# Attention with an MLP behind it: only TensorE's instructions kept in the order of the source, and the MLP's groups dealt out by TensorE's time

## The chip, the core and the metric

The kernel runs on one core of a Trainium2 chip. A core has five engines that run side by side, each with its own queue of instructions in a fixed order: TensorE (PE; its weight loads are shown apart, as PEld), VectorE (DVE), ScalarE (ACT), GpSimd (POOL) and SyncE (SP), whose queue here does nothing but issue transfers. An instruction waits by semaphores for what it needs, and all that stand behind it on its engine wait with it. The metric is the time of one execution on the device, in microseconds.

## The reference

Eight batches, eight heads of width 64, 576 positions. Attention is causal by blocks of 64 positions; its output, with the heads side by side (576 x 512), goes through a gated MLP with a layer norm and a mixing over positions.

```python
scores = np.matmul(q, k.transpose(0, 1, 3, 2)) / np.sqrt(D)
scores = np.where(block_i >= block_j, scores, -1e9)          # blocks of 64
attn = np.exp(scores - scores.max(-1, keepdims=True))
attn = attn / (attn.sum(-1, keepdims=True) + 1e-9)
x = np.matmul(attn, v)                    # then heads side by side: (B, S, 512)
h = np.maximum(x @ w_in, 0.0)             # (B, S, 1024)
u, v = h[..., :512], h[..., 512:]
v_n = (v - mean(v)) / np.sqrt(var(v) + 1e-6)
v_s = np.einsum('ts,bsd->btd', w_spatial, v_n) + b_spatial[None, :, None]
return (u * v_s) @ w_out
```

## The kernel before

The kernel walks through 32 pairs of heads (8 batches of 4 pairs), and each pair through 7 slots. Slot 0 is the last 64 queries of both heads; slots 1 and 2 are query tiles 0 and 1 of the first and the second head, slots 3 and 4 tile 2, slots 5 and 6 tile 3. A step is one slot of one pair. The loop of steps writes the instructions of all engines in one order.

Products are made in a fast fp32 form with rounded inputs, and so each operand is split in two: hi is the rounded value (a cast on ScalarE, L244), lo the rest (a subtraction on GpSimd, L247). Three matmuls (hi by hi, hi by lo, lo by hi) stand for one. prep_pair splits the q and k of a pair, with two casts and then four pieces of lo. There is one buffer for the loaded data (`raw`), one for hi and one for lo. The pairs of batch 0 (the boot) are not split: their scores are full fp32, and their probabilities are turned over by TensorE (transposes_pe).

Of a split pair TensorE does, in this order: the scores of slots 0, 1 and 2 (L295, L283); MLP groups of the batch before; the scores of slots 3 to 6; the weighted-value product of the pair two before (av, L464 and L481, "AV" below); more MLP groups. The scores of a slot go through VectorE (row maximum, L318 and L327), ScalarE (exp, L334), VectorE (reciprocal of the sum, L345 and L348) and GpSimd (norm, L352). VectorE turns the probabilities over within blocks of 32 (transposes, L408) into a buffer `q`, and 16 transfers on SP's queue (move, L422) bring these blocks to their places in `turned`, of which there is one. av reads `turned`, so the next pair's moves wait for it to end.

AV gives x, in hi and lo (L439 on ScalarE, L443 on VectorE). When the four x of a batch are there, its MLP is put in a queue as groups of matmuls: v groups (mv, L512), u groups (mu, L606), sp groups (ms, the mixing over positions, L630) and out groups (mo, L664). Each has an evacuation and further work on the other engines, put off by later(steps, phase, ...) to a phase of a later step; due(phase) writes what has come due. `rate` is the number of groups over the number of steps, and each step that has a whole credit takes one group.

The splitting of a pair, and in batches 0 and 1 that of the weights, is background work: spread(generator, pieces, first, last) deals it out over steps.

What sets the order of each engine is own(): it pins each instruction behind the one pinned before it on the same engine. Every compute instruction is pinned. The transfers of SP are not: where they stand in its queue is decided by the tile scheduler, which puts instructions in the order in which it reckons that they can start.

Of the kernel before, what the change touches and what calls it, by code (L numbers as in the profile page):

```python
# [29 lines left out]
NS = len(SLOTS)  # L30
# [3 lines left out]
RUN2 = 3  # L34
AV_AT, BOOT_AV = 2 * NS + RUN2, NS + 5

# [6 lines left out]
def kernel(  # L43
# [10 lines left out]
    nc = tc.nc  # L54
# [5 lines left out]
    ND = DH // P  # L60
# [19 lines left out]
    def own(ins):  # L80

        tc.keep_in_program_order(ins)

# [350 lines left out]
    def x_evac(b, pr, av, q0, n):  # L434
        qs = slice(q0, q0 + n)

        def hi():
            x = x_tiles(b, pr)
            own(nc.scalar.copy(x[:, 0, qs], av[:, :n]))  # L439

        def lo():
            x = x_tiles(b, pr)
            own(nc.vector.tensor_tensor(  # L443
                out=x[:, 1, qs], in0=av[:, :n], in1=x[:, 0, qs].bitcast(F32), op=ALU.subtract
            ))

        later(1, 0, hi)
        later(1, 1, lo)

    def av(b, pr):  # L450
# [27 lines left out]
        for c in range(5):  # L478
# [9 lines left out]

        later(1, 2, lambda: own(nc.gpsimd.tensor_scalar(
            out=tails[b][:, pr], in0=xts[(b, pr)][:, :, FULL * P:].bitcast(F32), scalar1=1.0,  # L490
# [4 lines left out]
    def moe(b):  # L495
# [5 lines left out]
        def v_group(c):  # L501
# [89 lines left out]

            later(1, 0, evac)
            later(1, 2, stats)
            later(2, 1, scale)
            later(2, 2, normal)
            later(3, 2, rest)

        def u_group(z, dc):
# [17 lines left out]

            later(1, 0, evac)

# [3 lines left out]
        def sp_group(z, dc):  # L622
# [30 lines left out]

            later(1, 0, gate)
            later(1, 1, split_g)

        def out_group(z, ec):
# [16 lines left out]

            later(1, 0, leave)

        def groups(f, need, *args):
            return [(need, lambda a=a: f(*a)) for a in args]

        def free():  # L680
            return True

        vs = groups(v_group, free, *((c,) for c in range(FULL + 1)))
        us = groups(u_group, free, *((z, d) for z in range(2) for d in range(ND)))
        sps = [groups(sp_group, lambda: ready["v"] > FULL, *((z, d) for d in range(ND)))
               for z in range(2)]
        outs = [groups(out_group, lambda z=z: ready[z] == ND, *((z, e) for e in range(NO)))
                for z in range(2)]

        order = "vvuvuvuvuuuuu" if b else "v" * 5 + "u" * 8  # L690
        queue = [(vs if w == "v" else us).pop(0) for w in order]
# [59 lines left out]
    queue = []  # L751
    rate = 0.0
    credit = 0.0

# [12 lines left out]
    def begin(b):  # L767
        nonlocal rate
        queue.extend(moe(b))
        steps = NPAIR * NS + (0 if b else AV_AT - BOOT_AV)  # L770
        rate = len(queue) / steps if b < B - 1 else 1.0

    n = -1
    while n < N + NS or queue or todo:
# [5 lines left out]
        if here and g + 1 < len(pairs):  # L780
            b, pr = pairs[g + 1]
            if i == 0 and b > 0:
                load_pair(b, pr)
            if i == NS - 1 and b == 0 and pr > 1:
                load_v(b, pr)
            if n == 1:
                load_pair(0, 1)
                load_v(0, 1)
            if i == RUN2 + 1 and g + 2 < NPAIR:
                load_pair(0, g + 2)  # L790
            if i == RUN2 + 1 and b > 0:
                spread(prep_pair(b, pr), 6, n, n + 2)
        if i == 3 and NPAIR < g < len(pairs):
# [15 lines left out]
        for of in range(max(0, g - 2), min(g + 1, len(pairs))):  # L809
            b, pr = pairs[of]  # L810
            if n - of * NS == (BOOT_AV if by_pe((b, pr)) else AV_AT):
                av(b, pr)
                if pr == NPAIR - 1:
                    later(1, 3, lambda b=b: begin(b))

# [16 lines left out]
        step_background(n)  # L832
        if at(n - 4) and by_pe(at(n - 4)[:2]):
            for j in TURNS[(i - 4) % NS]:
                transposes_pe(*at(n - 4)[:2], j)
        credit = min(credit + rate, 2.0)
        while credit >= 1.0 and queue and queue[0][0]():
            queue.pop(0)[1]()
            credit -= 1.0
        due(2)  # L840
# [46 lines left out]
```

## Time and profile before

| | us |
|---|---|
| median of three runs | 800.57 |
| the three runs | 791.61, 800.57, 807.21 |
| the profiled execution | 797.51 |
| its span in the trace | 795.7 |
| granted TensorE clock over the span | 0.935 |

The profile is of one execution. A row of an engine gives its busy time, the share of the span and the number of instructions. A row of waits names who waited, for whom, the sum in us, the number of times and the longest. A row of a timeline begins with the start and the duration in us; in brackets stands how long the engine had been idle, and what ended it. The granted clock is a share of full speed. Names are those of the program: `s` scores, `p` probabilities, `q` the turned blocks, `lo` and `hi` the halves of q and k.

### The profile page before, as it was taken

The page shows a single profiled execution, that of the slowest core. Times are in us where ns is not written, and L with a number is a line of the kernel's source. Part 1 is how long each engine was busy: PE and PEld are TensorE (multiplying, and loading weights), DVE is VectorE, ACT ScalarE, POOL GpSimd, SP SyncE. Part 2 cuts the span into 40 slices and gives each one's busy share as a digit, 9 for nine tenths or more (in the row PEclk, how much of TensorE's full clock was granted, in tenths as well). Part 3 has the DMA queues.
Part 4 walks back from the last instruction along what each step waited for, and adds up shares of the span by engine and source line. Part 5 has one row for each costly group of instructions (what it writes and reads, how often), then busy time and mean ns, then how long its engine had stood idle before and what let it go on. Part 6 is the DMA issues. An engine that isn't in the chain of part 4 may idle for free.

```text
span 795.7 us, 16364 instructions
## 1 busy us (share of the span) xinstructions
PE 715.7 (90%) x5729; PEld 635.5 (80%) x5729; DVE 465.2 (58%) x1587; ACT 426.4 (54%) x1156; POOL 342.6 (43%) x529
## 2 busy tenths in 40 slices
PE   8876968898988898998988899988988989899998
PEld 5554757787888787887878788887878988799898
DVE  5657877754774557745684557745675456731430
ACT  5775574443663457634763457634664437642542
POOL 4557467642444543344434543355344434341011
PEclk9997877989998999999998999999989889899999
DMA  7322445334444454345444354444544344431001
GB/s 259 123 72 93 128 126 157 88 116 136 124 116 130 127 157 112 105 123 146 130 130 130 101 165 115 113 115 139 152 129 102 97 121 132 98 99 36 26 1 60
DMA packets 42150, 92.05 MB, mean 116 GB/s; under 512 B 9298, under 2 KB 18002, under 8 KB 42068
## 3 DMA queue, kind: packets, MB, share of 16 engines
q1 hardware_dynamic: 32852, 81.56, 37.8%
q10 hardware_dynamic: 9216, 9.44, 3.5%
q8 instruction: 45, 0.74, 0.4%
q14 instruction: 37, 0.30, 0.1%
HBM read 38.18 MB, written 9.44 MB: 60 GB/s over the span
## 4 chain that ended last, share of the span: by engine, by line
PE 66%; POOL 13%; DVE 9%; issue 5%; ACT 4%; DMA 2%; SPq 1%; POOLq 0%; DVEq 0%; ACTq 0%
PE mo L664 10%; PE ms L630 10%; PE mu L606 10%; PE s L283 9%; PE mv L512 9%; POOL lo L247 7%; PE avh L464 6%; POOL p L352 4%; PE s L295 3%; PE avl L464 3%; DVE p L318 2%; PE avh L481 2%; DVE q L408 2%; ACT p L334 1%; PE t L380 1%
## 5 line engine op out<-in xcount | busy, mean ns | idle before, releaser
L334 ACT ACTIVATE p<-p,nmax 128x384 f32<-128x384 f32 (+4 forms) x288 | 167.3, 582 | 207.0 <-DVE nmax L318 97.0
L352 POOL TENSOR_SCALAR p<-p,ssum 128x384 f32<-128x384 f32 (+4 forms) x288 | 161.5, 575 | 197.9 <-DVE ssum L348 166.0
L247 POOL TENSOR_TENSOR lo<-raw,hi 128x288 fp32r<-128x288 f32 x112 | 95.3, 872 | 110.4 <-issue 89.0
L318 DVE CUSTOM_DVE_ANT_0 p<-s,mask 128x128 f32<-128x128 f32 (+3 forms) x256 | 117.3, 481 | 21.0 <-PE t L380 13.9
L606 PE MATMUL mu<-x,wi_hi 128*128 128x288 f32 x512 | 119.9, 316 | 0.0
L408 DVE STREAM_TRANSPOSE q<-p 128x384 f32<-128x384 f32 (+1 forms) x189 | 108.6, 612 | 16.7 <-POOL p L352 8.2
L649 POOL TENSOR_TENSOR gl<-u,gh 128x288 fp32r<-128x288 f32 x64 | 51.7, 809 | 110.5 <-ACT gh L648 110.5
L639 DVE TENSOR_TENSOR u<-ms,u 128x288 f32<-128x288 f32 x64 | 29.2, 456 | 116.2 <-PE ms L635 116.2
L606 PEld LDWEIGHTS mu<-x,wi_hi 128*128 128x128 f32 x512 | 91.9, 204 | 3.7 <-issue 0.9
L512 PE MATMUL mv<-wi_hi,x 128*128 128x512 f32 x256 | 84.5, 397 | 0.0
L630 PE MATMUL ms<-ws_hi,vh 128*128 128x288 f32 x256 | 82.7, 323 | 0.2 <-ACT q L386 0.2
L630 PE MATMUL ms<-ws_lo,vh 128*128 128x288 f32 x256 | 79.6, 311 | 0.0
L630 PE MATMUL ms<-ws_hi,vl 128*128 128x288 f32 x256 | 79.6, 311 | 0.0
L664 PE MATMUL mo<-gh,wo_hi 128*128 128x288 f32 x256 | 77.8, 304 | 0.0
L664 PE MATMUL mo<-gl,wo_hi 128*128 128x288 f32 x256 | 76.8, 300 | 0.0
L664 PE MATMUL mo<-gh,wo_lo 128*128 128x288 f32 x256 | 76.7, 299 | 0.0
L295 PE MATMUL s<-hi,lo 128*128 128x288 f32 x56 | 22.3, 399 | 59.4 <-POOL lo L247 59.4
L606 PE MATMUL mu<-x,wi_lo 128*128 128x288 f32 x256 | 75.4, 314 | 0.0
L295 PEld LDWEIGHTS s<-hi,lo 128*128 128x128 f32 x56 | 12.7, 227 | 64.5 <-POOL lo L247 64.5
L512 PEld LDWEIGHTS mv<-wi_hi,x 128*128 128x128 f32 x256 | 48.4, 189 | 10.8 <-issue 0.6
L630 PEld LDWEIGHTS ms<-ws_hi,vh 128*128 128x128 f32 x256 | 52.4, 205 | 3.0 <-issue 1.3
L334 ACT ACTIVATION_READ_ACCUMULATOR p<-p,nmax 128x1 f32 x288 | 54.3, 189 | 0.0
(118 smaller groups left out, 1620.7 us busy)
## 6 DMA issues: line engine op xcount, KB each, us to landing
turned<-q SPq DMA_DIRECT2D x216, 100.0 KB, 2.2
turned<-q SPq DMA_DIRECT2D x216, 96.0 KB, 2.2
raw<-qk SPq DMA_DIRECT2D x31, 608.0 KB, 4.1
v<-v SPq DMA_DIRECT2D x32, 320.0 KB, 4.3
outT<-o ACTq DMA_DIRECT2D x64, 144.0 KB, 1.8
rwi<-w_in SPq DMA_DIRECT2D x8, 512.0 KB, 4.3
rwo<-w_out SPq DMA_DIRECT2D x4, 512.0 KB, 4.4
rws<-w_spT SPq DMA_DIRECT2D x4, 288.0 KB, 3.1
```

What stands on the lines that cost most here:

```text
L247: own(nc.gpsimd.tensor_tensor(out=lo[:, cs], in0=raw[:, cs], in1=hi[:, cs].bitcast(F32), op=ALU.subtract))
L283: own(nc.tensor.matmul(banks[(b, pr, i + hd)][:, o:o + n], a[js, qs], k[js, :n], start=(m == 0), stop=(m == len(parts) - 1),))
L295: own(nc.tensor.matmul(bk[z][:, :HT], a[:, Q8:], k[:, z * HT:(z + 1) * HT], start=(m == 0), stop=(m == len(parts) - 1),))
L318: own(nc.vector.tensor_tensor_reduce(out=pt[:, o:o + n], in0=bk[:, o:o + n], in1=mask[:, 512 - n:], scale=-0.125, scalar=BIG, op0=ALU.add, ...
L334: own(nc.scalar.activation(pt[:, o:o + n], pt[:, o:o + n], AF.Exp, bias=mx, scale=-1.0, accum_out=ssum[:, s0 + r:s0 + r + 1],))
L352: own(nc.gpsimd.tensor_scalar(out=pt[:, o:o + w], in0=pt[:, o:o + w], scalar1=ssum[:, r:r + 1], scalar2=1.0, op0=ALU.mult, op1=ALU.mult,))
L408: own(nc.vector.transpose(to[:, :, o:o + 32 * n].rearrange("p r (c j) -> p c r j", j=32), pt[:, :n * P].rearrange("p (c r j) -> p c r j", ...
L464: own(nc.tensor.matmul(out[js, (t0 - q0) * P:(t1 + 1 - q0) * P].rearrange("p (t a j) -> p a t j", a=4, j=32), vt[:, c, js], src[:, :, o:o ...
L512: own(nc.tensor.matmul(ps, xs[k][:, j, cs], w[:, k, DH:], start=(n == 0), stop=(n == 3 * NC - 1),))
L606: own(nc.tensor.matmul(ps[:, :HT], w[:, k, ds], xs[k][:, j, zs], start=(n == 0), stop=(n == 3 * NC - 1),))
L630: own(nc.tensor.matmul(ps[:, :HT], a[:, ds], w[:, k, zs], start=(n == 0), stop=False))
L664: own(nc.tensor.matmul(ps[:, :HT], w[:, k, es], a[:, k, :], start=(n == 0), stop=(n == 3 * ND - 1),))
```

## The change

own() now pins only TensorE's instructions. The scheduler orders the four other engines, and SP's queue as before, by its own reckoning. TensorE's order is written a little differently too. MLP groups are dealt out by their length on TensorE: each has a number (in us), each step pays `pace` in, a group or a fixed part of a pair (PAIR_LENGTHS: scores of slots 0 to 2, scores of 3 to 6, AV) takes its length out. The phases of several evacuations move back by one, and so does the start of a batch's MLP. The first split pair, (1, 0), is prepared from slot 2 over four steps instead of from slot 4 over two. In the boot AV and the transposes come one step sooner, and one v group changes places with a u group.

```diff
-AV_AT, BOOT_AV = 2 * NS + RUN2, NS + 5
+AV_AT, BOOT_AV = 2 * NS + RUN2, NS + 4
+
+PAIR_LENGTHS = (1.8, 1.45, 2.95)
...
     def own(ins):
 
-        tc.keep_in_program_order(ins)
+        if ins.ins.engine == mybir.EngineType.PE:
+            tc.keep_in_program_order(ins)
...
-        later(1, 0, hi)
-        later(1, 1, lo)
+        later(1, 1, hi)
+        later(1, 2, lo)
...
-            later(1, 0, evac)
+            later(1, 1, evac)
             later(1, 2, stats)
             later(2, 1, scale)
             later(2, 2, normal)
-            later(3, 2, rest)
+            later(3, 1, rest)
...
-            later(1, 0, gate)
-            later(1, 1, split_g)
+            later(1, 1, gate)
+            later(1, 2, split_g)
...
-        vs = groups(v_group, free, *((c,) for c in range(FULL + 1)))
-        us = groups(u_group, free, *((z, d) for z in range(2) for d in range(ND)))
+        vs = groups(v_group, 2.75, free, *((c,) for c in range(FULL + 1)))
+        us = groups(u_group, 1.6, free, *((z, d) for z in range(2) for d in range(ND)))
...
-        order = "vvuvuvuvuuuuu" if b else "v" * 5 + "u" * 8
+        order = "vvuvuvvuuuuuu" if b else "v" * 5 + "u" * 8
...
-        rate = len(queue) / steps if b < B - 1 else 1.0
+
+        pace = (sum(q[2] for q in queue) + sum(PAIR_LENGTHS) * steps / NS) / steps
...
-            if i == RUN2 + 1 and b > 0:
-                spread(prep_pair(b, pr), 6, n, n + 2)
+            if i == (2 if boot else RUN2 + 1) and b > 0:
+                spread(prep_pair(b, pr), 6, n, n + (4 if boot else 2))
...
-                    later(1, 3, lambda b=b: begin(b))
+                    later(2, 1, lambda b=b: begin(b))
...
-        if at(n - 4) and by_pe(at(n - 4)[:2]):
-            for j in TURNS[(i - 4) % NS]:
-                transposes_pe(*at(n - 4)[:2], j)
-        credit = min(credit + rate, 2.0)
-        while credit >= 1.0 and queue and queue[0][0]():
-            queue.pop(0)[1]()
-            credit -= 1.0
+        if at(n - 3) and by_pe(at(n - 3)[:2]):
+            for j in TURNS[(i - 3) % NS]:
+                transposes_pe(*at(n - 3)[:2], j)
+        if here and not boot and i in (0, RUN2):
+            owed -= PAIR_LENGTHS[0] if i == 0 else PAIR_LENGTHS[1]
+        if i == RUN2 and NPAIR + 1 < g < len(pairs):
+            owed -= PAIR_LENGTHS[2]
+        owed = min(owed + pace, 3.0)
+        while owed > 0.0 and queue and queue[0][0]():
+            _, group, length = queue.pop(0)
+            group()
+            owed -= length
```

How this moves instructions is seen in the built programs. In the rows below a name carries batch, pair and slot: p_4_2_3 is the probabilities of batch 4, pair 2, slot 3. Lines of the changed kernel are three higher than before.

The first place is the split of pair (4, 3), done during pair (4, 2). ScalarE's row of instructions before, from the exp of slot 3 on:

```order
L334 ACTIVATE p_4_2_3_4925,ssum_4_2_3_4924<-p_4_2_3_4925,nmax_4_2_3_4923 128x384
L566 ACTIVATE vr_3_2_4814<-vr_3_2_4814,st_3_2_4815 128x512
L574 CAST vh_3_2_4947<-vr_3_2_4814 128x512
L439 CAST x_4_0_4950<-avl_4_0_4880 128x256
L439 CAST x_4_0_4950<-avh_4_0_4881 128x320
L530 ACTIVATE vr_3_3_4932<-mv_3_3_4931 128x512
L334 ACTIVATE p_4_2_4_4960,ssum_4_2_3_4924<-p_4_2_4_4960,nmax_4_2_4_4959 128x384
L244 CAST hi_4_3_4965<-raw_4_3_4736 128x576
L244 CAST hi_4_3_4965<-raw_4_3_4736 128x640
```

and in the changed kernel:

```order
L337 ACTIVATE p_4_2_3_4924,ssum_4_2_3_4923<-p_4_2_3_4924,nmax_4_2_3_4922 128x384
L569 ACTIVATE vr_3_2_4813<-vr_3_2_4813,st_3_2_4814 128x512
L337 ACTIVATE p_4_2_4_4940,ssum_4_2_3_4923<-p_4_2_4_4940,nmax_4_2_4_4939 128x384
L577 CAST vh_3_2_4932<-vr_3_2_4813 128x512
L247 CAST hi_4_3_4948<-raw_4_3_4736 128x576
L247 CAST hi_4_3_4948<-raw_4_3_4736 128x640
L442 CAST x_4_0_4944<-avl_4_0_4879 128x256
L337 ACTIVATE p_4_2_5_4977,ssum_4_2_5_4976<-p_4_2_5_4977,nmax_4_2_5_4975 128x512
L442 CAST x_4_0_4944<-avh_4_0_4880 128x320
```

The two casts of hi_4_3 stood behind the x of the AV and an evacuation of a v group (vr_3_3); now they stand right behind the exp of slot 4 and a cast of vh, ahead of both. GpSimd at the same place before:

```order
L247 TENSOR_TENSOR lo_4_3_4966<-raw_4_3_4736,hi_4_3_4965 128x288 x2
L489 TENSOR_SCALAR xs_4_4951<-x_4_0_4950 128x128
L352 TENSOR_SCALAR p_4_2_3_4925<-p_4_2_3_4925,ssum_4_2_3_4924 128x384
L352 TENSOR_SCALAR p_4_2_4_4960<-p_4_2_4_4960,ssum_4_2_3_4924 128x384
L247 TENSOR_TENSOR lo_4_3_4966<-raw_4_3_4736,hi_4_3_4965 128x288
L247 TENSOR_TENSOR lo_4_3_4966<-raw_4_3_4736,hi_4_3_4965 128x352
```

and in the changed kernel:

```order
L355 TENSOR_SCALAR p_4_2_3_4924<-p_4_2_3_4924,ssum_4_2_3_4923 128x384
L355 TENSOR_SCALAR p_4_2_4_4940<-p_4_2_4_4940,ssum_4_2_3_4923 128x384
L250 TENSOR_TENSOR lo_4_3_4949<-raw_4_3_4736,hi_4_3_4948 128x288 x3
L250 TENSOR_TENSOR lo_4_3_4949<-raw_4_3_4736,hi_4_3_4948 128x352
L355 TENSOR_SCALAR p_4_2_5_4977<-p_4_2_5_4977,ssum_4_2_5_4976 128x512
```

The four pieces of lo_4_3 stood two and two around the tail's copy (xs) and two norms; now the norms come first and all four pieces follow.

The second place is SP's queue one pair earlier. Before, from the last moves of q_4_0 on:

```order
L422 DMA turned_122<-q_4_0_4310 32x800 x2
L422 DMA turned_122<-q_4_0_4310 32x768 x2
L234 DMA raw_4_3_4736<-qk 128x1216
L256 DMA v_4_1_4861<-v 128x640
L422 DMA turned_122<-q_4_1_4593 32x768
```

and in the changed kernel, up to the first moves of q_4_0:

```order
L259 DMA v_4_0_4567<-v 128x640
L237 DMA raw_4_3_4736<-qk 128x1216
L425 DMA turned_122<-q_4_0_4322 32x768
L425 DMA turned_122<-q_4_0_4322 32x800 x2
L425 DMA turned_122<-q_4_0_4322 32x768
```

The load of raw_4_3 stood behind all sixteen moves of q_4_0; now it stands ahead of them.

The third place is VectorE at the end of pair (4, 2), up to the first row maximum of pair (4, 3), nmax_4_3_0. Before:

```order
L582 TENSOR_TENSOR vl_3_3_5025<-vr_3_3_4932,vh_3_3_5024 128x512
L536 TENSOR_TENSOR vr_3_4_5013<-mv_3_4_5012,vr_3_4_5013 64x512
L539 TENSOR_SCALAR vr_3_4_5013<-vr_3_4_5013 64x512
L542 BN_STATS st_3_4_5014<-vr_3_4_5013 64x6
L543 BN_AGGR st_3_4_5014<-st_3_4_5014 64x2
L546 TENSOR_SCALAR st_3_4_5014<-st_3_4_5014 64x1
L408 STREAM_TRANSPOSE q_4_2_4914<-p_4_2_3_4925 128x3x4x32
L408 STREAM_TRANSPOSE q_4_2_4914<-p_4_2_4_4960 128x3x4x32
L345 TENSOR_SCALAR ssum_4_2_5_4997<-ssum_4_2_5_4997 128x2
L348 RECIPROCAL ssum_4_2_5_4997<-ssum_4_2_5_4997 128x2
L327 ISA p_4_3_0_5090,nmax_4_3_0_5088<-s_4_3_0_0_5060,mask_93 128x288
```

and in the changed kernel:

```order
L411 STREAM_TRANSPOSE q_4_2_4913<-p_4_2_6_5011 128x4x4x32
L545 BN_STATS st_3_3_4956<-vr_3_3_4955 128x6
L546 BN_AGGR st_3_3_4956<-st_3_3_4956 128x2
L549 TENSOR_SCALAR st_3_3_4956<-st_3_3_4956 128x1
L539 TENSOR_TENSOR vr_3_4_4991<-mv_3_4_4990,vr_3_4_4991 64x512
L555 TENSOR_SCALAR st_3_3_4956<-st_3_3_4956 128x1
L542 TENSOR_SCALAR vr_3_4_4991<-vr_3_4_4991 64x512
L559 TENSOR_SCALAR st_3_3_4956<-st_3_3_4956 128x1
L545 BN_STATS st_3_4_4992<-vr_3_4_4991 64x6
L563 TENSOR_SCALAR st_3_3_4956<-st_3_3_4956 128x1
L546 BN_AGGR st_3_4_4992<-st_3_4_4992 64x2
L330 ISA p_4_3_0_5074,nmax_4_3_0_5072<-s_4_3_0_0_5044,mask_93 128x288
```

Before, the statistics of one v group (st_3_4) and two transposes of slots 3 and 4 came ahead of it; now the last transpose of the pair (slot 6) and the statistics of two v groups (st_3_3, st_3_4) do.

## What the change should do to the time

> **What bounds the kernel now.** I read the totals and the chain of waits first, since they say which engine to follow, and then the waits of that engine.
>
> ```profile
> span 795.7 us, 16364 instructions
> PE 715.7 (90%) x5729; PEld 635.5 (80%) x5729; DVE 465.2 (58%) x1587; ACT 426.4 (54%) x1156; POOL 342.6 (43%) x529
> PE 66%; POOL 13%; DVE 9%; issue 5%; ACT 4%; DMA 2%; SPq 1%; POOLq 0%; DVEq 0%; ACTq 0%
> PE s L295 <- POOL lo L247: 61.5, 26, 4.8
> PE avl L464 <- DMA turned<-q: 2.2, 1, 2.2
> ```
>
> TensorE is busy for 90% of the span, and of its 80 us of idle time 61.5 us are one wait: the first scores of a split pair wait for GpSimd's low halves, in 26 places. The transfers into `turned` cost it 2.2 us in all. So the time can fall by about 10% and no more, unless the matmuls themselves become faster, and the windows by stage (length, busy time of PE, its weight loads, DVE, ACT and POOL, granted clock, DMA share, GB/s) say that they can, a little.
>
> ```profile
> 0.00:57.10 57.10, 48.03 (x347) 31.36 (x347) 32.38 (x134) 37.73 (x109) 27.71 (x52) 1.00 0.46 152
> 57.10:130.20 73.10, 56.10 (x358) 46.17 (x357) 57.20 (x171) 45.25 (x116) 46.09 (x56) 0.81 0.42 117
> 130.20:683.50 553.30, 505.17 (x4189) 457.10 (x4189) 340.83 (x1181) 297.98 (x821) 246.20 (x390) 0.94 0.46 126
> 683.50:795.70 112.20, 106.35 (x839) 100.83 (x837) 34.81 (x103) 45.48 (x113) 22.60 (x34) 0.97 0.17 48
> ```
>
> I cut the span where pairs begin: A is the boot batch with the first three split pairs (to 130.2), B the 24 pairs from there (553.3 us, 92.2 us for each four pairs), C the last pair and the tail. In A's second part and in B the granted clock is 0.81 and 0.94. The next rows show what a lost clock looks like: a wait for the low half, then matmuls at 0.44 us where such ones take 0.29.
>
> ```profile
> 249.01 0.61 PE L295 MATMUL s<-hi,lo 128*128 128x288 f32 x1 [2.32 <-POOL lo L247]
> 254.41 0.44 PE L630 MATMUL ms<-ws_lo,vh 128*128 128x288 f32 x1
> 255.90 0.29 PE L630 MATMUL ms<-ws_hi,vh 128*128 128x288 f32 x1
> 249.00:256.00 7.00, 6.99 (x34) 6.49 (x35) 1.39 (x6) 1.19 (x3) 2.84 (x4) 0.53 0.55 165
> 273.60:280.60 7.00, 6.99 (x54) 6.46 (x54) 4.17 (x18) 2.86 (x10) 3.58 (x5) 1.00 0.57 182
> ```
>
> A seven-microsecond stretch behind the 2.32 us wait ran at 0.53, another, behind a wait as long, at 1.00: the loss follows some of the waits. In B it is 0.06 x 553 = 33 us.
>
> One batch in full, and its first pair, where TensorE's weighted-value product (AV) starts at 304.74:
>
> ```profile
> 295.30:384.40 89.10, 81.76 (x706) 74.00 (x705) 56.39 (x198) 50.12 (x138) 40.06 (x64) 0.98 0.47 127
> 318.35 0.40 PE L295 MATMUL s<-hi,lo 128*128 128x288 f32 x1 [2.39 <-POOL lo L247]
> 339.48 0.40 PE L295 MATMUL s<-hi,lo 128*128 128x288 f32 x1 [2.32 <-POOL lo L247]
> 362.66 0.40 PE L295 MATMUL s<-hi,lo 128*128 128x288 f32 x1 [2.63 <-POOL lo L247]
> 304.74 0.87 PE L464 MATMUL avl<-turned,v 128*64 128x256 f32 x8
> 310.73 0.60 ACT L530 ACTIVATE vr<-mv 128x512 f32<-128x512 f32 x1 [1.45 <-PE mv L512]
> 311.22 0.61 ACT L334 ACTIVATE p<-p,nmax 128x384 f32<-128x384 f32 x1
> 311.82 1.29 ACT L244 CAST hi<-raw 128x576 fp32r<-128x576 f32 x2
> 313.24 1.57 POOL L247 TENSOR_TENSOR lo<-raw,hi 128x288 fp32r<-128x288 f32 x2 [5.42 <-issue]
> 315.06 1.14 POOL L352 TENSOR_SCALAR p<-p,ssum 128x384 f32<-128x384 f32 x2
> 316.17 2.12 POOL L247 TENSOR_TENSOR lo<-raw,hi 128x288 fp32r<-128x288 f32 x2
> 307.63 10.07 SPq L422 DMA_DIRECT2D turned<-q  x16
> 318.32 0.33 SPq L234 DMA_DIRECT2D raw<-qk  x1
> ```
>
> Less its three waits (7.3 us) and 0.02 x 89.1 = 1.8 us of clock, the batch is 80.0 us, 20.0 us a pair: the floor of TensorE's own work. The reader is to see why the low half is late. ScalarE waits in the order of the source at 310.73 for a matmul of the MLP; behind it stand an exp and the cast of the high half, which only needs data loaded long ago. GpSimd stood idle 5.42 us, then did two pieces, the norms, and two more. The low half is complete at 318.29, 13.55 us after AV began; the next pair's scores wanted it 2.39 us before they started.
>
> **The change part by part.** Only TensorE keeps the source's order, so the scheduler places all else, and the order rows above show the result at three places. *The split (ScalarE, GpSimd).* The casts stand behind the exp of slot 4, and the four pieces of the low half behind the norms of that exp, ahead of the copy of the tail. The work is the same; the rows below have its price.
>
> ```profile
> L247 POOL TENSOR_TENSOR lo<-raw,hi x112: 786/810/1382, 55.5 to 684.6; 128x288 fp32r<-128x288 f32 x84, 128x352 fp32r<-128x352 f32 x28
> 328.38 0.61 ACT L334 ACTIVATE p<-p,nmax 128x384 f32<-128x384 f32 x1 [0.97 <-POOL p L352]
> 326.57 0.87 PE L464 MATMUL avl<-turned,v 128*64 128x256 f32 x8
> ```
>
> With T the start of AV (326.57 in a pair with few ScalarE evacuations), the exp of slot 3 starts at T + 1.8. With 0.6 us for each of the exps of slots 3 and 4, 1.3 us for the casts and 3.3 us for four pieces, the low half can end between T + 7 and T + 8. In the pair with the MLP's v groups I put it 4 us ahead of now (the exp at 311.22 goes where the 1.45 us wait and the evacuations ahead of it stood), T + 9.6. The next scores come at T + 11.2 (318.35 - 2.39 - 304.74), so the waits at L295 go: 2.4 us in three pairs of four.
>
> *SP's queue.* The 16 transfers of a pair into `turned` stood ahead of the next pair's load of q and k, and now stand behind it. That load overwrites `raw`, so it waits for the low half's end (now 318.32 behind 318.29); the transfers, which were free to go once AV had ended (307.63), now queue behind that wait.
>
> ```profile
> L422 SPq DMA_DIRECT2D turned<-q x432: 507/590/1865, 87.4 to 710.1; - x144
> DMA to landing us min/median/max: 2.0/2.2/4.4
> L234 SPq DMA_DIRECT2D raw<-qk x31: 327/515/617, 3.1 to 664.0; - x31
> ```
>
> From the low half's end to the next AV there are then 0.5 (the load's issue), 10.1 (sixteen issues), 2.2 (landing) and about 0.4 of semaphores: 13.2 us. So AV to AV takes at least the low half's end plus 13.2: 20.2 to 21.2 us in quiet pairs against TensorE's own 20.0, and 22.8 in the v pair. This new wait is what the floor does not get: 2.8 us in one pair of a batch, and 0.1 to 1.2 in the others, of which I take 0.3 each.
>
> *VectorE.* At a batch's third pair the v groups' statistics and the last transposes now stand ahead of the next pair's first row maxima. One statistics instruction takes 0.69 us by its row; the order shows two of these, two passes over 64 rows and six short ones ahead of the maxima. At 0.69 for each of the four long ones they can make the maxima, and with them the banks for scores 3 to 6, 2 to 3 us late.
>
> ```profile
> L542 DVE BATCH_NORM_STATS2 st<-vr x40: 678/686/697, 87.6 to 760.0; 128x6 f32<-128x512 f32 x32, 64x6 f32<-64x512 f32 x8
> ```
>
> It meets the AV wait of the same pair, so I count 4 us for the two together, bounded by 2.8 (one hides the other) and 5.8 (none does).
>
> *The clock.* Between nothing (no wait left behind which it drops) and all 33 us of B. The waits of 2.3 us and more behind which it drops become waits of under 2, but for the ones at the batch's one bad pair, so I take 1 us a batch. [...]
>
> *Groups by TensorE's time.* No work goes or comes; later phases move some evacuations by one step, which the four banks of the MLP's results cover, 0 us; without that cover each late evacuation costs TensorE one of 0.6 us (the row at 310.73). One u group (12 matmuls at 0.316 by the page, 1.6 us paced) moves past 683.5: B less 1.6, C plus 1.6.
>
> *Boot and first split pair.* The split of pair (1, 0) starts two steps sooner and is spread over four.
>
> ```profile
> 62.39 0.61 PE L295 MATMUL s<-hi,lo 128*128 128x288 f32 x1 [4.84 <-POOL lo L247]
> 104.89 0.40 PE L295 MATMUL s<-hi,lo 128*128 128x288 f32 x1 [4.16 <-POOL lo L247]
> 116.04 0.79 PE L283 MATMUL s<-hi 64*128 64x512 f32 x1 [1.97 <-DVE nmax L318]
> ```
>
> The 4.84 us wait goes; of 4.16 I count 3.5 since GpSimd no longer splits weights there, 1 of a shorter wait in pair (1, 1), 1 of the 1.97. The clock loss of the second part is 0.19 x 73.1 = 13.9, of which I take half, 7. Against that, in the boot ScalarE's cast and GpSimd's low half now stand ahead of the last exps and norms of batch 0: between 0 and 8 us (two times one load and its split, 4.1 us for the load by the page's row of DMA issues), and I take 3.
>
> ```profile
> raw<-qk SPq DMA_DIRECT2D x31, 608.0 KB, 4.1
> ```
>
> **The sum.** A: 3 - 4.8 - 3.5 - 1 - 1 - 7 = -14. B: a batch is 80.0 + 4 + 1 (three times 0.3) + 1 (clock) = 86 for 92.2, so six times -6.2 = -37, and -1.6. C: 2.4 of one wait, 1.5 of clock, + 1.6: -2.3. Together -55, so a span of 741 for 795.7. The profiled execution's own time was 797.5, its span plus 1.8, and so I forecast **743 us**; the median of the runs shown is 800.6, 3 us above that execution, well inside the runs' 791.6 to 807.2.
>
> **The rivals.**
> 1. All waits vanish: the low half ends at T + 7 everywhere and VectorE's lateness is covered. A batch takes about 81, so 5 us less in each of six: 713. For it: TensorE's idle time has one main cause. Against: the order of SP's queue. 17%.
> 2. New waits take most of it: the low half ends at T + 10 in every pair, AV to AV is 23.2 by the chain above, and a batch is 90 to 92: 24 to 36 us above the forecast, 767 to 779, and up to 790 with boot dear. For: the transfers now hang on the slowest piece of the split. Against: the quiet pair's rows. 13%.
> 3. The clock stays slow in spite of shorter waits: 743 plus 27 in B and some in A, 773. [...] 10%.
> 4. The change does not do what it says: the pieces still end late, since the exps ahead of the cast wait for VectorE. Only A gains: 785 to 795. Against: the 5.42 us in which GpSimd was idle. 5%.
> 5. Slower: a transfer's issue is dearer behind a load in flight. Now one costs 10.07 / 16 = 0.63 us; the row's median is 0.59, its longest 1.87. The chain from AV to AV is 7.5 + 3.1 + 16 times the issue, and it reaches today's 23.05 us a pair at 0.78 us. To be slower by 2% (16 us) in spite of what A and C gain (16), B must lose 32: 97.5 us a batch, 24.4 a pair, an issue of 0.86. Against: sixteen transfers right behind a weight load took no more than 10.45.
>
> ```profile
> 123.14 0.33 SPq L141 DMA_DIRECT2D rwo<-w_out  x1
> 123.59 10.45 SPq L422 DMA_DIRECT2D turned<-q  x16
> ```
>
> This gets 5%.
>
> That leaves 50% for my forecast, whose own range is 725 to 765. The range for 8 in 10 reaches to the first rival below and through the second and third above: 710 to 788. About 2% is what a measurement of this kernel can tell from no change. Faster by over 2% (under 784.5) are the forecast, rivals 1 and 3, and nearly all of rival 2: 85%. Within it are rival 4 and the rest of rival 2: 10%. Slower: 5%.
>
> **What would show it.** Right: L295's wait for the low half falls from 61.5 us to under 15; the wait of L464 for `turned` rises from 2.2 to 10 or 30; the granted clock in the middle passes 0.97; the transfers start right behind the load of q and k and that right behind the low half's end. VectorE's maxima become the wait of scores 3 to 6 once a batch. Wrong: a clock still at 0.94 beside short waits (rival 3); AV waits in every pair of over 2 us (rival 2); low halves that end later than T + 10 (rival 4); or issues of over 0.75 us (rival 5).

## The result and the profile after

| | before | after |
|---|---|---|
| median of the runs, us | 796.43 (4 runs) | 742.57 (4 runs) |
| lowest to highest | 791.61 to 807.21 | 739.95 to 745.51 |
| span of the profiled execution | 795.7 | 741.5 |
| granted clock over the span | 0.935 | 0.968 |

The ratio is 0.934, with a 95% interval from 0.926 to 0.943. The forecast was 743 us. The number came out; the experiments below show that one of the reasons given for it does not hold, and that the parts of the sum agree less well than the sum.

The page of the changed kernel, and TensorE's largest waits there:

```profile
span 741.5 us, 16390 instructions
PE 683.2 (92%) x5729; PEld 606.8 (82%) x5729; DVE 454.0 (61%) x1587; ACT 421.9 (57%) x1156; POOL 350.0 (47%) x529
PE 35%; DVE 22%; ACT 19%; POOL 9%; issue 6%; DMA 5%; SPq 3%; DVEq 0%; ACTq 0%; POOLq 0%
PE s L286 <- DVE nmax L321: 10.0, 10, 3.8
PE avl L467 <- ACT p L337: 8.0, 5, 2.0
PE avl L467 <- DMA turned<-q: 7.1, 4, 2.9
PE s L298 <- POOL lo L250: 6.1, 3, 3.2
PE ms L633 <- ACT u L618: 5.3, 4, 1.4
```

The wait for the low half fell from 61.5 us to 6.1. In its place stand several smaller ones, of which AV's (L467) make 15.1 in the two rows. The first row, VectorE's row maxima, lies mostly in the boot (7.9 us); in the 24 middle pairs it is small:

```profile
PE s L286 <- DVE nmax L321: 1.8, 6, 0.3
```

TensorE's busy time fell by 32.5 us with the same 5729 matmuls, as the granted clock rose from 0.935 to 0.968: by the shares that it falls short of 1, 0.065 x 795.7 and 0.032 x 741.5, I estimate 28 of the 32.5 us for the clock. The chain that ended last no longer runs along TensorE for 66% of the span but for 35%, and through VectorE and ScalarE for 41%.

The windows of the changed kernel, cut where the first matmul of pairs (1, 0), (1, 3) and (7, 3) starts (columns as before):

```profile
0.00:61.80 61.80, 48.75 (x346) 32.66 (x347) 41.66 (x148) 41.52 (x116) 42.45 (x63) 0.83 0.53 175
61.80:117.77 55.97, 46.96 (x360) 39.20 (x359) 43.26 (x156) 40.02 (x107) 32.45 (x45) 0.91 0.40 112
117.77:630.15 512.38, 481.75 (x4179) 435.04 (x4177) 335.46 (x1179) 294.95 (x821) 254.51 (x391) 0.98 0.51 135
630.15:741.50 111.35, 105.70 (x853) 99.94 (x851) 33.61 (x105) 45.40 (x114) 20.55 (x32) 1.00 0.18 50
290.39:376.17 85.78, 81.56 (x707) 74.03 (x705) 55.59 (x197) 49.65 (x138) 41.00 (x64) 0.98 0.51 135
```

By the same cut the kernel before has 129.4, 553.9 and 112.5 us for the stages A, B and C; now they are 117.8, 512.4 and 111.4. The last row is one batch: 85.8 us, of which TensorE works 81.6.

### The profile page after: what moved, and what is told of

It is laid out like the page before. It is cut to its first block, busy times and chain, and to the rows that moved or that the text cites. A ratio compares the mean times of both kernels' runs of the same rounds, so it can differ in the third digit from the quotient of the medians.

```text
span 741.5 us, 16390 instructions
## 1 busy us (share of the span) xinstructions
PE 683.2 (92%) x5729; PEld 606.8 (82%) x5729; DVE 454.0 (61%) x1587; ACT 421.9 (57%) x1156; POOL 350.0 (47%) x529
## 4 chain that ended last, share of the span: by engine, by line
PE 35%; DVE 22%; ACT 19%; POOL 9%; issue 6%; DMA 5%; SPq 3%; DVEq 0%; ACTq 0%; POOLq 0%
PE ms L633 9%; ACT p L337 8%; PE mo L667 8%; DVE q L411 6%; DVE p L321 4%; POOL p L355 4%; PE avh L467 4%; ACT vr L569 4%; PE mv L515 3%; DVE st L545 3%; PE mu L609 3%; POOL lo L250 2%; PE s L286 2%; SPq L425 2%; DMA outT<-o 2%
## 5 line engine op out<-in xcount | busy, mean ns | idle before, releaser
L355 POOL TENSOR_SCALAR p<-p,ssum 128x384 f32<-128x384 f32 (+4 forms) x288 | 171.1, 606 | 266.5 <-DVE ssum L351 71.9
L411 DVE STREAM_TRANSPOSE q<-p 128x384 f32<-128x384 f32 (+1 forms) x189 | 116.2, 623 | 32.3 <-POOL p L355 27.8
L609 PE MATMUL mu<-x,wi_hi 128*128 128x288 f32 x512 | 111.3, 301 | 2.4 <-DVE ssum L348 1.6
L609 PEld LDWEIGHTS mu<-x,wi_hi 128*128 128x128 f32 x512 | 85.0, 190 | 6.2 <-DVE ssum L348 1.9
L633 PE MATMUL ms<-ws_hi,vh 128*128 128x288 f32 x256 | 76.6, 299 | 5.3 <-ACT u L618 5.3
L633 PE MATMUL ms<-ws_hi,vl 128*128 128x288 f32 x256 | 75.3, 294 | 0.0
L633 PE MATMUL ms<-ws_lo,vh 128*128 128x288 f32 x256 | 75.3, 294 | 0.0
L651 ACT CAST gh<-u 128x288 fp32r<-128x288 f32 x64 | 27.1, 432 | 81.1 <-DVE u L642 77.2
L609 PE MATMUL mu<-x,wi_lo 128*128 128x288 f32 x256 | 70.4, 297 | 0.0
L348 DVE TENSOR_SCALAR ssum<-ssum 128x2 f32<-128x2 f32 (+2 forms) x128 | 24.6, 192 | 70.6 <-ACT p L337 70.3
```

What stands on the lines that cost most here:

```text
L355: own(nc.gpsimd.tensor_scalar(out=pt[:, o:o + w], in0=pt[:, o:o + w], scalar1=ssum[:, r:r + 1], scalar2=1.0, op0=ALU.mult, op1=ALU.mult,))
L411: own(nc.vector.transpose(to[:, :, o:o + 32 * n].rearrange("p r (c j) -> p c r j", j=32), pt[:, :n * P].rearrange("p (c r j) -> p c r j", ...
L609: own(nc.tensor.matmul(ps[:, :HT], w[:, k, ds], xs[k][:, j, zs], start=(n == 0), stop=(n == 3 * NC - 1),))
L633: own(nc.tensor.matmul(ps[:, :HT], a[:, ds], w[:, k, zs], start=(n == 0), stop=False))
```

## The experiments

All times are medians, and each ratio (with its 95% interval) is to the kernel before on the same chip. A, B and C are the three stages of one profiled execution by the cut above; executions of one kernel differ by some us, so a few us between two kernels say little.

| kernel | us | ratio | A | B | C |
|---|---|---|---|---|---|
| before | | | 129.4 | 553.9 | 112.5 |
| after | 742.6 | 0.934 (0.926 to 0.943) | 117.8 | 512.4 | 111.4 |
| TensorE alone pinned, nothing else | 767.9 | 0.969 (0.965 to 0.973) | 120.3 | 537.2 | 109.3 |
| all of the change, every engine pinned | 741.6 | 0.936 (0.933 to 0.940) | 117.2 | 508.8 | 114.9 |
| dealing by time alone | 750.6 | 0.946 (0.936 to 0.956) | 128.4 | 507.7 | 113.7 |
| later phases alone | 761.2 | 0.956 (0.950 to 0.963) | 134.5 | 511.5 | 113.1 |
| pinned, boot's edits undone | 751.8 | 0.946 (0.940 to 0.951) | 127.1 | 510.9 | 112.3 |
| before, waits filled with matmuls | 779.5 | 0.984 (0.981 to 0.988) | 127.7 | 539.2 | 109.8 |
| after, transfers ahead of the load | 738.4 | 0.932 (0.929 to 0.936) | 118.1 | 506.9 | 111.3 |
| pinned, split a step sooner | 736.0 | 0.925 (0.920 to 0.931) | 116.5 | 505.7 | 112.9 |

### Which part of the change carries it

The kernel before with only own() changed:

```diff
-        tc.keep_in_program_order(ins)
+        if ins.ins.engine == mybir.EngineType.PE:
+            tc.keep_in_program_order(ins)
```

> The kernel before with nothing changed but that only TensorE's instructions are pinned. Theory (the free order of ScalarE and GpSimd is what ends TensorE's wait for the low half): the wait of L295 for GpSimd falls from 61.5 us to under 15, the clock in the middle rises to 0.97 or more, and the time is 740 to 765. Rival (the dealing of the groups by TensorE's time, the later phases and the earlier first split are needed for it): the wait stays above 40 us and the time is 780 or more.

Its stage B, and TensorE's two largest waits over the whole span:

```profile
120.27:657.45 537.18, 496.14 (x4190) 445.71 (x4189) 337.58 (x1174) 296.03 (x819) 247.87 (x386) 0.97 0.48 129
PE ms L631 <- DVE x L444: 22.4, 6, 5.2
PE s L284 <- DVE nmax L319: 14.9, 18, 4.3
```

Neither theory. The wait for the low half is gone and the clock is 0.97, as the theory had it, but the time fell by 3% only. TensorE now waits in six places, up to 5.2 us each, at the first sp groups (L631).

The changed kernel with every engine pinned again (own() as before, all else kept):

> The changed kernel with every engine's compute instructions pinned again, all else of the change kept. Theory: the waits for the low half come back to 40 us or more and the time is within 2% of before, 785 to 815. Rival (the dealing does it): 740 to 765.

```profile
PE s L297 <- POOL lo L249: 40.5, 26, 4.6
117.19:625.99 508.80, 483.38 (x4179) 438.01 (x4177) 345.58 (x1177) 296.98 (x819) 245.39 (x388) 0.97 0.51 138
```

My theory failed here. The wait for the low half does come back, to 40.5 us (in B to 24.2, where the kernel before has 46.2), and the time is still that of the changed kernel: 741.6 against 742.6. On top of the rest of the change, the free order is worth nothing that can be measured. So I took the rest apart, all engines pinned: the dealing of the groups alone (lengths, `pace`, and the order of v and u, which differs from batch 1 on), and the later phases alone.

```diff
...
-        credit = min(credit + rate, 2.0)
-        while credit >= 1.0 and queue and queue[0][0]():
...
+        owed = min(owed + pace, 3.0)
+        while owed > 0.0 and queue and queue[0][0]():
...
```

> The kernel before with the dealing of the MLP's groups by TensorE's time alone (lengths, pace, the order of v and u groups); all engines pinned, phases and boot as before. Theory P (the later phases bring the low half forward, since exps and casts then stand ahead of evacuations): waits of 40 us or more, 775 to 800. Rival D (the dealing alone gives the kernel its gain, by putting TensorE's work where it waited): 745 to 765.

```diff
...
-            later(1, 0, evac)
+            later(1, 1, evac)
...
```

> The kernel before with the later phases alone (evacuations, x, gate, tails, the start of a batch's MLP); all engines pinned, dealing by count and boot as before. Theory P: the low half ends 1 to 3 us sooner, by T + 9.5 to T + 11.5, the waits for it fall to about half, and the time is 745 to 770. Rival D: within 2% of before, 780 to 805.

Each takes B from 553.9 to 508 or 512 by itself, so theory P failed for the dealing and rival D for the phases. Stage B before, with the dealing alone and with the phases alone, and the wait for the low half in B in the same order:

```profile
129.38:683.25 553.87, 505.32 (x4190) 457.07 (x4189) 341.62 (x1184) 297.85 (x821) 246.77 (x390) 0.94 0.46 126
128.36:636.08 507.72, 485.97 (x4200) 439.91 (x4201) 353.25 (x1188) 301.05 (x827) 250.22 (x392) 0.97 0.51 138
134.47:645.97 511.50, 481.25 (x4191) 435.76 (x4189) 346.29 (x1183) 298.24 (x821) 248.06 (x388) 0.98 0.51 138
PE s L295 <- POOL lo L247: 46.2, 21, 3.1
PE s L297 <- POOL lo L249: 21.1, 14, 3.5
PE s L295 <- POOL lo L247: 28.0, 18, 3.2
```

About half of each gain is waiting that is gone, the other half busy time of TensorE that got shorter as the clock in B rose from 0.94 to 0.97 and 0.98: of the 46.2 us of the dealing 19.4 are busy time (505.32 to 485.97), of the 42.4 us of the phases 24.1.

How the split stands to AV in a quiet pair, first before (AV at 326.57), then with the dealing alone (AV at 334.37):

```profile
330.99 0.37 ACT L439 CAST x<-avl 128x256 fp32r<-128x256 f32 x1 [1.91 <-PE mu L606]
331.57 0.43 ACT L615 ACTIVATE u<-mu 128x288 f32<-128x288 f32 x1
332.48 1.31 ACT L244 CAST hi<-raw 128x576 fp32r<-128x576 f32 x2
334.37 0.87 PE L466 MATMUL avl<-turned,v 128*64 128x256 f32 x8
337.74 0.62 ACT L336 ACTIVATE p<-p,nmax 128x384 f32<-128x384 f32 x1
338.35 1.29 ACT L246 CAST hi<-raw 128x576 fp32r<-128x576 f32 x2
339.78 1.57 POOL L249 TENSOR_TENSOR lo<-raw,hi 128x288 fp32r<-128x288 f32 x2 [2.66 <-issue]
342.70 1.72 POOL L249 TENSOR_TENSOR lo<-raw,hi 128x288 fp32r<-128x288 f32 x2
344.29 0.30 PE L297 MATMUL s<-hi 128*128 128x288 f32 x1
```

The cast starts 4.0 us after AV, where the quiet pair before had 5.9 and the pair with v groups that the prediction shows 7.1; the first piece of the low half starts at T + 5.4 in each of the four pairs of this batch, for T + 7.4 to 8.5 in the kernel before. In the pair shown the low half ends at T + 10.05, just as the scores come (T + 9.9); in other pairs it is still late, which makes the 21.1 us. GpSimd still does two pieces, the norms, two pieces. What is gone is the evacuation (u, at 331.57) that stood ahead of the exp and the cast and, like the x ahead of it, waited for the matmuls: in the source AV's length is now paid for, so no group is dealt in AV's own step, and the evacuation of the next one is written behind the cast. The later phases reach the same from the other side: they leave the dealing as it was and write the evacuation behind the exps. In a batch of that kernel (AV from 292.23 on) the low half ends at T + 11.3 to T + 11.7 in three pairs and at T + 13.9 in the pair with v groups, which is no sooner than before; the T + 9.5 to T + 11.5 that I expected holds for two of the four, though the time came out as expected. The free order is a third way: with it alone TensorE waits for the low half no more. The three do not add up, since they take away the same wait. Neither the dealing nor the phases help the boot: it takes 61.2 and 65.3 us there, against 56.8.

The boot's edits were undone in the pinned kernel (AV and transposes one step later, first split pair from slot 4 over two steps):

> The changed kernel with all engines pinned and the three edits of the boot undone (AV and transposes one step later, the first split pair from slot 4 over two steps). Theory (the gain lies in the 24 middle pairs, and the boot's edits are worth the 4.8 us wait of the first split pair at most): 742 to 750. Rival (the boot's edits carry 10 us or more): 752 or more.

It took 751.8, 10 us more than with them (by the ratios, which allow for the chip, 0.946 for 0.936, some 7 us). In the profiled execution A is 9.9 us longer (127.1 for 117.2), all of it in the boot itself (60.6 for 50.2). That is between the two and nearer to the rival: they carry more than the 4.8 us of one wait. Which of the three carries it was not taken apart.

### The clock

In the kernel before, 18 matmuls that are overwritten were put ahead of each split pair's first scores:

```diff
         for z in range(2):
+            if b > 0 and z == 0:
+                hi = parts[0][0]
+                for _ in range(18):
+                    own(nc.tensor.matmul(
+                        bk[z][:, :HT], hi[:, Q8:], hi[:, :HT], start=True, stop=True
+                    ))
```

> The kernel before, with 18 more matmuls (128 x 288, hi by hi, 2.4 us at full clock) ahead of each split pair's first scores, into the bank that these scores then overwrite: TensorE works through the time in which it waited for the low half, and the low half comes no sooner. Theory (the clock falls because TensorE idles there): the granted clock in the middle rises from 0.94 to 0.98 or more, and the time falls by 15 to 35 us, to 765 to 785. [...]

```profile
127.74:666.98 539.24, 533.97 (x4622) 488.14 (x4621) 343.88 (x1185) 297.92 (x821) 247.81 (x390) 1.00 0.48 130
```

The clock in B went from 0.94 to 1.00 and the time down by 1.6%, though TensorE does 432 more matmuls there and the low half comes no sooner by design. The 1.6% are less than the 2% that the prediction takes as the least that can be told, but the whole interval (0.981 to 0.988) lies below 1. The loss of clock was the idling: of B, TensorE idled for 48.6 us before and for 5.3 here. The gain, 12 us, is below the 15 to 35 expected. That the added matmuls (some 2.4 us a pair by my estimate, 18 at the 0.133 us from start to start that matmuls of this size take at a clock of 1.00 in the kernel before, from 257.37 to 258.83) also stand in pairs that waited little or not at all would explain it; this was not tested.

### What took the place of the wait

In the changed kernel one AV of each batch follows the chain that the prediction worked out. The low half of one pair, SP's queue behind it, and AV to AV:

```profile
195.97 0.87 PE L467 MATMUL avl<-turned,v 128*64 128x256 f32 x8
201.26 3.26 POOL L250 TENSOR_TENSOR lo<-raw,hi 128x288 fp32r<-128x288 f32 x4
204.55 0.33 SPq L237 DMA_DIRECT2D raw<-qk  x1
204.99 10.71 SPq L425 DMA_DIRECT2D turned<-q  x16
217.65 0.87 PE L467 MATMUL avl<-turned,v 128*64 128x256 f32 x8 [1.55 <-ACT p L337]
```

The low half ends at 204.52 (T + 8.55), the load goes 0.03 us later, the transfers end at 215.70, and AV starts at 217.65: 13.13 us after the low half, for 13.2 in the prediction. In the five batches where this can be followed it is 12.5 to 13.5, and AV waits there for 0.9 to 2.0 us. AV waits once more in each of these batches, for 0.6 to 1.7 us, and there it comes 14.1 to 15.2 us behind the low half: this second wait is longer than the chain accounts for. The profile names an exp of ScalarE as the releaser, but AV does not read it. To see which of the two it is, the transfers and the loads of the split pairs were pinned in the order of the source, transfers first:

```diff
-            nc.sync.dma_start(raw, qk[b, pr])
+            ld = nc.sync.dma_start(raw, qk[b, pr])
+            if b > 0:
+                tc.keep_in_program_order(ld)
...
-            nc.sync.dma_start(turned[32 * r:32 * r + 32, a, :w], t[32 * a:32 * a + 32, r, :w])
+            tc.keep_in_program_order(nc.sync.dma_start(
+                turned[32 * r:32 * r + 32, a, :w], t[32 * a:32 * a + 32, r, :w]
+            ))
```

> The changed kernel with the transfers into turned and the loads of the split pairs' q and k pinned in the order of the source, so that the transfers stand ahead of the load again. Theory (AV waits because the transfers queue behind a load that waits for the low half): the waits of L467 fall from 21 us to under 6, AV to AV goes to 20.0 or less in quiet pairs, and the time falls by 12 to 20 us, to 722 to 731. Rival (AV waits for an evacuation by ScalarE, as the profile names it in 5 of its waits): the waits stay and the time is 738 to 748.

Stage B and TensorE's waits in it:

```profile
118.11:625.05 506.94, 478.60 (x4179) 431.02 (x4177) 337.78 (x1177) 294.70 (x821) 253.73 (x391) 0.99 0.51 137
PE avl L471 <- DMA turned<-q: 6.1, 6, 2.9
PE avl L471 <- ACT p L339: 1.2, 1, 1.2
PE ms L637 <- DVE x L450: 7.7, 6, 1.6
PE avh L471 <- ACT u L622: 6.4, 5, 1.3
```

AV's waits in the two rows fell from 15.1 to 7.3 us, those named after ScalarE from 8.0 to 1.2: they were the transfers. The wait behind the chain shown is gone in every batch; of the second one 0.6 to 0.7 us are left. AV to AV is now 19.2 to 20.6 us in three pairs of a batch, but 24.5 in the fourth. The time, 738.4, is the rival's and not the 722 to 731 of the theory, although the theory had the cause; by the ratios (0.932 and 0.934) it cannot be told from the changed kernel's. In the profiled execution B fell by 5.4 us only, since other waits grew: AV's second half (avh, L471) now waits 6.4 us for 0.3, and the sp groups (L637) 7.7 for 5.3.

The pinned kernel has a wait for the low half left in B (24.2 us). It was to be taken away by writing the split from slot 3 and in one step:

```diff
-            if i == (2 if boot else RUN2 + 1) and b > 0:
-                spread(prep_pair(b, pr), 6, n, n + (4 if boot else 2))
+            if i == (2 if boot else RUN2) and b > 0:
+                spread(prep_pair(b, pr), 6, n, n + (4 if boot else 1))
```

> The changed kernel with all engines pinned, and the split of a pair written one step sooner (from slot 3, right behind its scores) and in one step, so that casts and low half stand ahead of the exp of slot 4, of the norms of slots 3 and 4 and of x. Theory (what is left of that kernel's time over TensorE's floor in the 24 middle pairs is the wait for the low half, 3.6 us a batch): the wait there falls from 27 us to under 4 and the time is 712 to 725. Rival (the norms and transposes, now later, take the place of that wait, as the transfers did in the changed kernel): 735 to 748.

Stage B, TensorE's two largest waits in it, the batch's third pair and the sums of a batch:

```profile
116.50:622.16 505.66, 481.50 (x4179) 434.32 (x4177) 343.16 (x1175) 294.87 (x818) 250.59 (x388) 0.99 0.51 138
PE s L285 <- DVE nmax L320: 10.1, 12, 1.2
PE mu L608 <- DVE x L445: 7.1, 6, 1.3
356.21:381.17 24.96, 21.96 (x169) 18.78 (x167) 18.64 (x62) 16.66 (x44) 8.84 (x14) 0.93 0.39 103
sum 84.78, PE 81.78 PEld 73.91 DVE 57.07 ACT 49.89 POOL 40.70; mean PE 20.45 PEld 18.48 DVE 14.27 ACT 12.47 POOL 10.18
```

The wait went, and B fell from 508.8 to 505.7, not by the 20 us of the theory: waits for VectorE's maxima (L285) and at the first u groups (L608) took its place, and the time, 736.0, is the rival's. The row before the last is the pair of a batch in which the MLP begins: in 25 us ScalarE works 16.7 and VectorE 18.6. The last row sums a batch of this kernel: 84.78 us, of which TensorE works 81.78. But for the free order alone and the filled waits, every version ends at 505 to 512 us for B, whatever its waits are called; here, with 481.50 of work and nearly full clock, some 24 us are left, four a batch. Which instruction in that pair would have to move to get them was not found.

### Two versions that try to beat both

The boot of the changed kernel is slower than before, 61.8 against 56.8 us. Two waits in its boot, and what follows them:

```profile
29.32 1.65 PE L286 MATMUL s<-raw 64*128 64x128 f32 x6 [3.83 <-DVE nmax L321]
46.01 1.65 PE L286 MATMUL s<-raw 64*128 64x128 f32 x6 [3.67 <-DVE nmax L321]
28.00:34.00 6.00, 4.67 (x17) 2.62 (x17) 5.33 (x22) 4.21 (x12) 3.83 (x6) 0.50 0.30 96
47.00:59.00 12.00, 9.98 (x40) 5.38 (x39) 6.57 (x26) 6.83 (x21) 8.69 (x12) 0.51 0.42 126
```

Behind each wait stands a stretch at about half clock, 0.50 behind the 3.83 us and 0.51 behind the 3.67. Pinned, the boot takes 49 to 50 us, but the three pairs behind it take 67 instead of 56. Two kernels join the better parts: the changed one with the transfers ahead of the load and all engines pinned in the boot, and the pinned one with the early split, freed for these three pairs.

```diff
-        if ins.ins.engine == mybir.EngineType.PE:
+        if now[0] < 4 * NS or ins.ins.engine == mybir.EngineType.PE:
             tc.keep_in_program_order(ins)
...
```

> The changed kernel with all engines pinned in the boot batch only (28 steps), free behind it, and the transfers into turned and the loads of the split pairs pinned in the order of the source. Theory (the free order costs the boot 10 us, since the split of weights and of the first split pair goes ahead of batch 0's own chain, and gains as much in the three pairs behind it): the boot takes 49 to 52 us, the three pairs 54 to 58, the rest as with the transfers first, together 723 to 730. Rival (what is not done in the boot must be done behind it, so that the sum of both stays at 117): 735 to 742.

```diff
-        if ins.ins.engine == mybir.EngineType.PE:
+        if not 4 * NS <= now[0] < 7 * NS or ins.ins.engine == mybir.EngineType.PE:
             tc.keep_in_program_order(ins)
...
```

> The kernel with the split written one step sooner and all engines pinned, but for the three split pairs behind the boot, in which only TensorE is. Theory as for the boot pinned: 49 + 56 + 506 + 113, together 722 to 729. Rival: the weights' split, not the order, is what those three pairs wait for, and the sum of boot and three pairs stays at 116: 733 to 738.

They took 738.2 us (0.925, 0.918 to 0.932) and 734.1 (0.919, 0.911 to 0.928), short of what was expected. Boot and three pairs of the first:

```profile
0.00:49.16 49.16, 43.79 (x347) 30.49 (x347) 35.23 (x135) 36.92 (x108) 29.03 (x54) 1.00 0.53 177
49.16:113.89 64.73, 50.91 (x360) 42.99 (x358) 55.88 (x169) 44.30 (x116) 46.68 (x56) 0.84 0.42 121
```

Both times lie in the ranges of the rivals: most of what the boot does not do, the three pairs must. The sum is 113.9, against 117.8, and 115.0 in the second kernel. VectorE has 55.9 us of work in these 64.7, where the changed kernel has 43.3 in 56.0.

The second was set against the changed kernel on one chip:

> The changed kernel once more, beside the next run on the same chip, so that the two can be set against each other: 738 to 746.

> The kernel with the early split, pinned but for the three split pairs behind the boot, once more. Theory (it saves some 3 us ahead of pair (1, 3) and 6 in the 24 middle pairs): 731 to 737, under the changed kernel by 0.7% to 1.5%. Rival (the earlier difference lay between chips): within 0.5% of the changed kernel.

744.4 us (0.935, 0.932 to 0.939) and 734.0 us (0.923, 0.919 to 0.927): 1.4% under the changed kernel on the same chip. That is less than 2%, but the six runs of the one (732.2 to 738.2) and of the other (741.9 to 745.7) do not overlap. Its median is the lowest of all; from the kernel with the early split and all engines pinned (0.925, 0.920 to 0.931) it cannot be told.

## Why the prediction was right, and where it was not

- **The bound, right.** TensorE's wait for the low half and the clock that it costs were what could be had. A batch's floor of 80.0 us holds: the batch of 84.8 us in the kernel with the early split has 3.0 us of waits and 1.7 of lost clock (0.07 x 24.96), which leaves 80.1.
- **The sum, right by stages.** A: -11.6 for -14 (boot +5.0 for +3, the three pairs -16.6 for -17.3). B: -41.5 for -38.6. C: -1.1 for -2.3. Together -54.2 for -55.
- **The terms within a batch, right in total and in part by luck.** The batch shown (85.8 us) has 4.2 us of waits and 1.7 of lost clock (0.07 of the 24.6 us of its first pair), for 4.9 and 1 in the sum. VectorE's lateness, put at 2 to 3 us once a batch, cost 0.3, so that it and the AV wait of that pair came to 2.3 us for 4. Against that, a second AV waited 1.7 us, where the sum had 0.3, and the clock lost more.
- **The new wait in SP's queue, right** in mechanism and size at one AV of each batch: 13.13 us for 13.2, and with the transfers pinned ahead of the load that wait went. The 0.4 us of semaphores in its chain was an estimate; in the rows shown the load goes 0.03 us behind the low half, the first transfer 0.11 us behind the load's issue, and AV 0.35 us behind the last landing (2.2 us after that transfer's issue began at 215.11). In these pairs, the ones with v groups, the low half ends at T + 8.6 to T + 8.8, for T + 9.6 in the prediction, and in the quiet ones mostly ahead of its T + 7 to T + 8. My later expectation that 12 to 20 us could be had there was wrong: 5.4 us came in B.
- **The clock, right.** It rose with the waits gone (0.94 to 0.98 in B), and filling the waits raised it as well (to 1.00). Rival 3 (the clock stays slow in spite of shorter waits) is refuted for this kernel: its 27 us in B are the 33 us of lost clock less the 6 that the sum keeps, and the changed kernel loses 0.02 x 512.4 = 10 us there. That a wait of under 2 us costs no clock, on which the 1 us a batch of the sum rests, does not hold throughout: behind AV's wait of 1.96 us the changed kernel ran at 0.64 from 303.29 to 308.00.
- **Wrong: the step "Groups by TensorE's time", put at 0 us,** and with it the whole credit given to the free order. The dealing alone is worth 46 us in B, the later phases alone 42, the free order alone 17, and on top of the other two nothing. So the low half comes early in the changed kernel, as the sum needs, but not only by the edit that I credited: without the free order the time is the same. I had read the blocked evacuation at 310.73 rightly and then counted only the part that frees the engine which is blocked. The two others take the blocker away. A blocked queue can be cured at the queue, at what is written ahead, or at what the blocker waits for, and each such edit had to be priced for itself.
- **Too small: the boot's edits.** Undone in the pinned kernel they cost 10 us in A, all in the boot; in the sum they stood with the 4.8 us of one wait, and 3 us against, and AV and the transposes one step sooner had no term. The two boot waits, with the clock at 0.50 and 0.51 behind them, were not foreseen.

The second rival (new waits take most) was partly there: some four to five us a batch stay above the floor, even in the versions whose B ends at 505 to 512 us.

## What to carry to other kernels

When several edits attack one wait, price each alone and expect the gains to overlap: here edits worth 46, 42 and 17 us in the middle stage together gave 41. Before freeing an order, look for what blocks it: here it was enough to write an evacuation one phase later, or to deal the groups by the time that they take. A removed wait is worth its length only until the next chain is reached, here some 4 us a batch above the floor.

## What the runs showed of the hardware

The granted clock halved behind some of TensorE's waits of 2.3 us (0.53 in the stretch that the prediction shows; 1.00 behind another wait of 2.6). 504 matmuls that compute nothing of use, 432 of them in B, made the kernel 1.6% faster, with the clock in B at 1.00 where it was 0.94.

Behind the load of q and k the sixteen transfers shown took 10.71 us to issue, for 10.07 ahead of it. Over all pairs the issues are as long as before and the landings later. The two rows of the changed kernel, and the landings when the transfers stand ahead of the load again:

```profile
L425 SPq DMA_DIRECT2D turned<-q x432: 507/590/1954, 85.3 to 656.1; - x144
DMA to landing us min/median/max: 2.0/2.6/6.0
DMA to landing us min/median/max: 2.1/2.2/4.1
```

Before, the issues were 507/590/1865 ns and the landings 2.0/2.2/4.4 us. So a load in flight hardly made an issue dearer (rival 5), but the median landing came 0.4 us later behind it (2.6 us for 2.2).
